# Sparse attention and a maxout layer on one core: a branch hint for ScalarE, an earlier check of the sums, and another order of work

## The chip, the cores and the metric

The kernel runs on one core of a Trainium2 chip. The metric is the device time of one execution, in microseconds; three runs of the kernel before gave 179.23, 179.29 and 179.44, and their median is the time before.

The core has a matrix engine (TensorE, PE in the profile; its weight loads are PEld), a vector engine (VectorE, DVE), an engine for functions of one operand (ScalarE, ACT), a general one (GpSimd, POOL) and one that issues transfers (SyncE, SP). Each has a sequencer of its own that takes its instructions in program order (PEq, DVEq, ACTq, POOLq and SPq in the profile). They meet through semaphores.

## The reference

Four batches of eight heads of 768 positions and 64 columns. Three heads see all earlier keys, the other five only the first four keys and the last 64. Then a layer of two products, the larger of both, and a third product:

```python
scores = scale * np.matmul(q, k.transpose(0, 1, 3, 2))
...
mask = np.where(retr[0, :, 0, 0, None, None], full_mask, stream_mask)
scores = np.where(mask[None, :, :, :], scores, -1000000000.0)
scores = scores - np.max(scores, axis=-1, keepdims=True)
a = np.exp(scores)
a = a / (np.sum(a, axis=-1, keepdims=True) + 1e-09)
return np.matmul(a, v).astype(np.float32)
...
h1 = x @ w1
h2 = x @ w2
g = np.maximum(h1, h2)
return (g @ w_out).astype(np.float32)
```

q, k, v and the result are float32; x has 3072 rows of 512, w1 and w2 are 512 x 1024, w_out is 1024 x 512.

## The kernel before

**Stages.** A batch is worked in two halves of 384 queries, in the order (batch, half) = (0,0), (1,0), (0,1), (1,1), (2,0), (2,1), (3,0), (3,1), and the eight heads of a batch in four pairs. For each half the loads bring q, k and v in float32. Casts (`cast_qk`, `cast_v`) make bfloat16 of them, picking the heads in an order that the chip works out from `is_retrieval` (`head_order`, L1578 to L1606) and keeps in registers. PE or a transposing DMA turns q and k (`turn`, L674), a copy takes them out (`unturn`). `mix_k` and `mix_v` lay out the first and the near keys of a window together (tiles `kx`, `vx`). Score tiles (`scores`, L953) go to PSUM, ACT takes the exponential (`exp`, L972), DVE the mask (`mask`, L991), PE the products with v and a column of ones that gives the row sums (`weighted`, L1016). `normalise` multiplies by the inverse sums (`rez`; L1033 and L1043) into the tile `x`, which is turned to `xt`.

The layer uses max(h1, h2) = relu(x (w1 - w2)) + x w2: `sub` makes w1 - w2 (L1178), w2 w_out is folded into one matrix on the chip (L1195 turns w2, L1222 multiplies), `up` makes x (w1 - w2) in eight groups of columns (L1245, four matmuls each), `relu` follows (L1270, L1272), and `down` adds x w2 w_out and the relu's product with w_out (L1302, three groups of four matmuls for a tile of 128 rows). A copy takes the tile out (`ot`) and a DMA stores it (L1327). The very last piece, 128 columns wide, is copied and stored by ACT, the others are stored by SP.

**Order.** All this is a list of 1094 numbered operations. The string `PLAN` says in which order they are emitted and on which engine: `1092p4` is operation 1092 on PE with PSUM bank 4, `v` is DVE, `a` ACT, `g` POOL, `s` SP, and `x0*3` are three warm-up matmuls on zeros into bank 0 (tile `warmer`, L366). Each engine takes its own operations in this order and waits, in order, for what they need.

**The numbers used below.** Loads on SP: 3 and 8 are the two halves of w2, 13 and 16 those of w1, 4, 6, 9 and 11 the four quarters of w_out. 52 is a cast of q and 38 one of v's rows in half (0,0). 237, 241, 244 and 249 are the first four score tiles of half (1,0), 174, 176, 188, 190, 202 and 204 their `mix_k`, 201 an `unturn`. 206, 208, 210, 212, 217, 219, 221 and 223 are the ups of half (0,0); 208 and 221 are the first, in the plan before and in the other, that need the half of w1 which is loaded last. 214 is a `down` group of it. 989 to 991 and 979 to 981 are `down` groups of half (3,0), 992 the copy behind 991. 1081 to 1088 end half (3,1), 1089 and 1090 are ACT's last copy and store.

**The check.** Operations 1091 to 1093 test that all inverse sums are sane and that three heads see everything: `judge` (four instructions on DVE), `total` (one matmul of one column on PE) and `say` (three on DVE), which writes `verdict`. Every engine loads `verdict` into a register and branches: with a verdict of 1 past `tile_any_heads`, a slow version that covers any heads and that this input does not need, to the end of the program. There the engines meet, SP waits for all semaphores one by one, and a barrier ends the program (both at L1727 of the profile). For some engines the branch has a hint: an instruction at their start that names the branch's target as likely.

Of the kernel before, what the change touches and what calls it, by code (L numbers as in the profile page):

```python
# [177 lines left out]
100p 94p3 101v 96p 104p0 102v 106p 14s 139p 103v 107v 138p 97v 109v 141p 98v 142p 108v 15s 99v 150p 126v 116p2
114p4 117a 151p 115v 134p6 137p 12v 217p0 130v 145p 218a 152p 146a 219p3 17s 118v 153a 223p2 220a 122v 221p4
224a 208p0 222v 18s 192a 180g 212p1 154a 164g 178v 209a 210p5 194v 156a 213v 184p3 160p2 211a 166v 198p4 185v  # L180
140p 143p 199v 21s 155a 167g 147p 165a 157g 179v 144a 195g 172p0 162p1 161v 170p5 181a 193g 206p3 19s 163a
173v 148a 200p4 174v 186p6 171a 237p21 201v 420s 241p07 187a 176v x5*2 204v x5*2 243a x5 207v 244p54 238a x6
249p67 188v 216p3 190v 245a 202v 250a 247v 242a 227p 239a 20s 251a 240v 234p 246a 252v 248v 421s 196a 182g
253p25 197a 158v 257p60 169a 159g 261p17 215p4 254a 168v 255a 203v 175v 265p2 177a 256v 259a 266p 270p5 226p
23s 258a 267v 205v 268v 262a 260v 183a 231p 263a 235a 191v 264v 271p 276p0 189v 232a 236s 281p 214p6 272v 269v
295a 289g 423s 282v 305v 306a 296g 275p1 284v 277p 225p 283v 315g 424s 274v 290g 309p7 316v 228p 310a 278v 22s
273v 279v 319p3 229a 311v 293p4 280v 299p2 320a 313v 294v 287p0 285p5 288a 323v 356p76 286v 422s 360p13 357a
363p40 321v 335p5 300v 361a 670s 450g 433a 337p7 441g 427v 442a 358a 325p1 301v 303v 434a 446v 24s 338a 359v
339p2 438g 326a 428v 331p6 365a 336v 340a 327p7 332v 449a 364a 333p1 454g 328v 669s 426a 439g 341p0 440v 432a
425g 362a 334v 329p5 547s 448v 431v 366p26 447v 330a 369p47 374p31 368a 550s 297v 307g 292v 429p5 370a 317g  # L190
451p6 291v 375a 435p4 298g 668s 371a 452v 342p 308g 430a 302g 343p 373v 312g 376a 453v 367a 393p3 394p 344a
304g 436v 395p 318a 396p 377p76 324a 322g 549s 381p51 372v 385p20 379a 346p4 383a 437v 380v 314v 386a 672s
397v 347p 399v 382a 398v 230s 378a 389p61 384v 233s 387a 348p 391a 388v 390a 400p2 401p 407p5 392v 402p 406p3
403v 351p7 803s 579a 568v 558g 404v 559a 405v 412p 578g 569a 408p 562p0 413v 409v 552a 673s 414v 352p 563a
415v 411v 548s 353p 553a 410v 349a 418p1 354a 556p6 350s 419v 416p2 557a 800s 486p50 417v 490p34 488a 493p71
443p6 491a 457p2 444v 495a 675s 459p0 494a 458v 487a 455p3 460v 671s 492a 469p1 445v 456v 345s 496p67 489v
470a 499p25 504p04 497a 507p31 501a 806s 523p6 564v 498a 524p 566v 503v 525p 506a 526p 467p5 551s 505a 527v
529v 509a 463p7 528v 500a 468v 461p4 807s 684g 677a 683v 700g 464a 465p0 510v 355s 462a 692g 476p1 508a 502v
699a 678g 688s 466v 511p62 691a 515p57 513a 519p43 477p 681s 555v 581g 517a 516a 580g 530p0 554g 560a 531p
518v 561g 696s 532p 521a 481p2 520a 533v 535v 570g 512a 482p 522v 695s 571a 514v 565a 537p7 542p 572p5 689v  # L200
585a 587g 543v 534v 536p3 802s 538p 545v 582p4 573a 539v 483p 544v 540v 583a 676s 574v 478p 541v 577a 484v
575a 619p60 546s 584v 623p75 479a 626p43 567v 586v 471p2 576v 620a 697v 625a 472p 628a 621a 687s 630v 473p
624a 622v 627a 631p16 703s 629v 635p53 632a 639p07 474v 652p4 633a 641a 647p1 634v 648p 643p62 640a 649v 653p
651v 645a 804s 594p7 654v 644a 650v 637a 596p0 656v 674s 636a 655v 600p2 646v 595a 638v 597a 598p6 682s 601a
642v 590p1 599a 602p3 591v 592p4 926s 603v 657p5 593a 659p 480s 588p7 660v 661v 614p0 485s 702a 701g 680v 693a
679g 475s 589a 685v 609p2 706g 686a 704s 662v 694a 690a 738p61 698g 742p34 739a 745p75 801s 610p 746a 743a
611p 747a 744a 799s 658p6 663p 615p 740a 664v 665v 612a 924s 741v 616p 705v 666v 748p73 617v 751p54 749a
756p12 667s 752a 759p60 604p7 760a 754v 758a 824v 834g 605p 805s 808a 809v 814a 825g 606p 613s 815v 835a 757a
812s 775p5 750a 607v 776p 753a 777p 778p 763p62 761a 755v 767p13 779v 765a 771p74 762v 782p0 781v 772a 828s
783p 780v 719p2 773a 768a 707p5 774v 813s 816g 720a 721p7 811v 826a 817g 810a 708v 715p4 827a 818s 836a 821g  # L210
722v 833a 733p1 716a 831v 837v 823a 819s 769a 717p2 843v 841a 770v 784p 713p5 764a 785v 718v 839s 789p7 714a
794p 787v 709p4 795v 766v 711p3 829s 710a 797v 796v 788p6 712a 790p 786v 723p2 608s 791v 820v 792v 838s 734p
822v 793v 840v 842v 875p54 925s 879p73 882p06 877a 735p 880a 881a 928s 832v 830v 876a 724p 883a 878v 725p 884a
885v 736a 886v 798s 903p4 726v 904p 887p73 891p50 905v 888a 895p61 906v 908p2 892a 907v 728p7 897a 927s 893a
899p54 729p 889a 894v 900a 932s 901a 890v 896a 730p 902v 727s 898v 909p 913p1 731v 915p 914p0 929s 854p3 916v
910v 917v 919p 865p5 912v 911v 930s 920v 848p4 855v 922v 844p6 931s 921v 849a 918v 858p7 845a 732s 850p2 859a
856p3 923s 955a 934v 956g 933a 852p0 857v 940g 947a 846p4 948a 938s 853a 870p1 851a 847v 939a 935v 949g 937s
871p 957v 936a 942a 958a 950v 872p 941v 954a 962v 946g 866p 873v 944s 867p 973p6 868a 943s 994p73 974v 998p02
995a 1001p41 975p5 952s 996a 945v 1003a 977p6 997v 1000a 951s 976v 965p7 1002a 971p3 999a 966v 978a 967p1 960s
972v 1004p25 968v 969p4 1006a 959s 953v 1005a 1007p07 970v 1012p63 1009a 1015p15 737s 1019p24 1008a 1011v  # L220
1031p7 874s 1017a 1032p 1010v 1033p 1014a 618s 1018v 1034p 961v 984p0 1013a 869s 1035v 1036v 1016a 1037v
# [1410 lines left out]
def kernel(  # L1632
# [13 lines left out]
    nc = tc.nc  # L1646
# [9 lines left out]
    with tc.tile_pool(name="consts", bufs=1) as consts:  # L1656
# [13 lines left out]
        if K_BY_ACT:  # L1670
# [7 lines left out]
            found, engines=[nc.gpsimd.engine, nc.vector.engine, nc.scalar.engine], min_val=0, max_val=H - 1,  # L1678
# [8 lines left out]
        right = nc.values_load(  # L1687
            verdict, min_val=0, max_val=1, skip_runtime_bounds_check_because="a product of two flags"
        )
# [42 lines left out]
```

## Time and profile before

| | us |
|---|---|
| median of three runs | 179.29 |
| the profiled execution | 179.4 |
| its span, first to last instruction | 177.7 |
| PE busy in it | 169.6 |
| ACT busy | 124.5 |
| DVE busy | 117.0 |
| POOL busy | 32.5 |

The span is what the trace shows; 1.7 us of the execution lie around it. Busy times count work on data, and not a sequencer's branches, loads of registers, waits and issues of DMAs. Those stand in the groups by line under the engine's name with a q. TensorE's granted clock is 0.995 of full speed as a mean over the span. A row of the timeline gives the start, the length, engine, line and operation, and in brackets the idle time before it and what ended that.

### The profile page before, as it was taken

The numbers are of one execution on the slowest core, as the hardware profiler recorded it, in microseconds if no ns is written. First come the engines' busy times: TensorE is split into PE (matmuls) and PEld (weight loads), VectorE is DVE, ScalarE is ACT, GpSimd is POOL, SyncE is SP. The second block draws the span as 40 slices with busy tenths as digits, with TensorE's granted clock in tenths as the row PEclk, the third lists the DMA queues.
The fourth block names the chain that finished last, engine by engine and source line by source line (L and its number), as shares of the span: only waits on it lengthen the run. The fifth ranks groups of instructions, "written<-read, shape, count | busy, mean of one in ns | idle before, by whom it ended". The sixth has DMA issues, their size and how long they took to land.

```text
span 177.7 us, 4887 instructions
## 1 busy us (share of the span) xinstructions
PE 169.6 (95%) x1781; PEld 102.6 (58%) x1781; DVE 117.0 (66%) x326; ACT 124.5 (70%) x279; POOL 32.5 (18%) x80
## 2 busy tenths in 40 slices
PE   7999999999999999999999999999999999999970
PEld 7855655655756656666566447555554566545440
DVE  5448799878898787776777175786855578503130
ACT  3598716999698999999996879948475877132210
POOL 6860200320427310071001122000030000000000
PEclk9999999999999999999999999999999999999998
DMA  5999999999899998995959997549993261333040
GB/s 133 334 373 386 392 375 325 221 309 281 217 251 246 267 310 214 243 247 74 154 117 250 209 186 196 71 115 223 226 252 71 66 220 66 76 131 118 4 160 28
DMA packets 76654, 36.14 MB, mean 203 GB/s; under 512 B 59090, under 2 KB 70610, under 8 KB 76626
## 3 DMA queue, kind: packets, MB, share of 16 engines
q1 hardware_dynamic: 76480, 35.73, 78.5%
q8 instruction: 15, 0.25, 0.6%
q14 instruction: 13, 0.11, 0.2%
q10 hardware_dynamic: 146, 0.07, 0.1%
HBM read 25.17 MB, written 6.29 MB: 177 GB/s over the span
## 4 chain that ended last, share of the span: by engine, by line
PE 78%; DMA 7%; DVE 5%; ACT 2%; POOL 2%; issue 2%; DVEq 0%; SPq 0%; POOLq 0%; ACTq 0%
PE ps L1302 34%; PE ps L1245 21%; PE ps L953 9%; PE ps L1016 7%; DMA ld<-in_moe_w_out_dram 6%; PE ps L1222 3%; PE ps L674 3%; DVE at L991 1%; ACT at L972 1%; PE ps L1142 1%; POOL qb L378 1%; DMA raw<-in_is_retrieval_dram 1%; ACT wob L376 1%; POOL tab L606 1%; DVE vx L378 1%
## 5 line engine op out<-in xcount | busy, mean ns | idle before, releaser
L972 ACT ACTIVATE at<-ps 128x512 bf16<-128x512 f32 (+2 forms) x134 | 64.0, 576 | 6.7 <-PE ps L953 6.4
L1302 PE MATMUL ps<-wob,g 128*128 128x512 bf16 (+2 forms) x200 | 45.7, 371 | 0.0
L1245 PE MATMUL ps<-xt,w 128*128 128x384 bf16 x256 | 45.2, 326 | 0.0
L1245 PEld LDWEIGHTS <-w 128*128 128x128 bf16 x256 | 24.1, 98 | 16.5 <-issue 0.6
L991 DVE TENSOR_TENSOR at<-at,tab 128x1024 bf16<-128x1024 bf16 (+5 forms) x49 | 24.7, 519 | 12.4 <-ACT at L972 11.8
L1302 PEld LDWEIGHTS <-g 128*128 128x128 bf16 x200 | 18.2, 98 | 19.4 <-issue 0.2
L1272 DVE TENSOR_SCALAR g<-ps 128x384 bf16<-128x384 f32 x31 | 16.9, 552 | 14.7 <-PE ps L1245 14.3
L1302 PE MATMUL ps<-w2o,xt 128*128 128x512 bf16 (+2 forms) x100 | 24.7, 371 | 0.0
L1270 ACT ACTIVATE g<-ps 128x384 bf16<-128x384 f32 x33 | 15.9, 509 | 12.0 <-PE ps L1245 11.9
L1043 DVE TENSOR_TENSOR x<-ps,rez 128x192 f32 x64 | 22.6, 354 | 1.6
L378 POOL CAST qb<-ld 128x384 bf16 (+1 forms) x28 | 12.4, 476 | 57.3 <-DVE x L1043 19.8
L1016 PEld LDWEIGHTS <-at 128*128 128x128 bf16 x477 | 18.0, 97 | 6.1 <-DVE at L991 1.0
L376 ACT COPY ot<-ps 128x512 f32<-128x512 f32 (+1 forms) x16 | 9.1, 576 | 16.4 <-PE ps L1302 15.4
L1016 PE MATMUL ps<-vb,at 128*128 128x65 bf16 x387 | 19.3, 193 | 0.3 <-DVE at L991 0.2
L953 PE MATMUL ps<-qk 64*128 64x128 bf16 (+1 forms) x330 | 19.1, 228 | 0.0
L953 PEld LDWEIGHTS <-qk 64*128 64x128 bf16 x330 | 12.1, 94 | 9.3 <-issue 7.0
L376 ACT CAST qb<-ld 128x384 bf16 (+1 forms) x35 | 13.7, 451 | 4.5 <-DMA ld<-in_q_dram 3.3
L1302 PEld LDWEIGHTS <-xt 128*128 128x128 bf16 x100 | 8.9, 98 | 8.1
L378 DVE COPY qk<-ps 128x384 bf16<-128x384 bf16 (+1 forms) x14 | 9.6, 696 | 4.0 <-PE ps L674 3.6
L378 POOL CAST vb<-ld 128x192 bf16 x18 | 6.3, 385 | 28.7 <-DMA ld<-in_v_dram 26.6
L378 DVE COPY ot<-ps 128x512 f32<-128x512 f32 (+1 forms) x9 | 6.1, 673 | 8.0 <-PE ps L1302 8.0
L674 PE MATMUL ps<-tab,qb 128*128 128x128 bf16 x120 | 9.6, 219 | 0.5 <-POOL qb L378 0.3
(76 smaller groups left out, 162.9 us busy)
## 6 DMA issues: line engine op xcount, KB each, us to landing
out_dram<-ot SPq DMA_DIRECT2D x23, 256.0 KB, 2.6
ld<-in_v_dram SPq DMA_DIRECT2D x21, 256.0 KB, 5.2
ld<-in_moe_w_dram SPq DMA_DIRECT2D x4, 1024.0 KB, 12.1
ld<-in_q_dram SPq DMA_DIRECT2D x5, 768.0 KB, 8.2
ld<-in_k_dram SPq DMA_DIRECT2D x5, 768.0 KB, 7.8
ld<-in_q_dram SPq DMA_DIRECT2D x9, 256.0 KB, 5.1
ld<-in_k_dram SPq DMA_DIRECT2D x9, 256.0 KB, 4.6
ld<-in_moe_w_out_dram SPq DMA_DIRECT2D x4, 512.0 KB, 11.0
```

The costliest lines, as they stand in the source:

```text
L376: nc.scalar.copy(out=out, in_=in_)
L378: eng[e].tensor_copy(out=out, in_=in_)
L674: nc.tensor.transpose(to[:, i], qbs[:, T["qb", n, hf] % NQB, t, i].rearrange("p h d -> p (h d)"), ident)
L953: nc.tensor.matmul(to.rearrange("p (i c) -> p i c", c=128), lhsT=lhsT, rhs=q_of(n, i, m)[rows], start=bk not in under, stop=True, skip_gro ...
L972: nc.scalar.activation(out=at[:, bk, 0:w], in_=bank(("ps", b, hf, t), part=bk)[:, 0:w], func=ACT.Exp, scale=scale,)
L991: eng[e].tensor_tensor(out=at, in0=at, in1=tbl, op=ALU.mult)
L1016: nc.tensor.matmul(po[:, hh, i - NT * hf, :], lhsT=ats[:, T["at", b, hf, t] % NAT, bk, e * 128:(e + 1) * 128], rhs=rhs, start=first, stop= ...
L1043: nc.vector.tensor_tensor(out=xs[:, HALVES.index((b, hf)) % NX, :, bass.ds(heads[2 * p + hh], 1), :], in0=po[:, hh, :, 0:D].unsqueeze(2), ...
L1245: nc.tensor.matmul(bank(key)[:, 0:HALF], lhsT=w[:, kc, fc * 128:(fc + 1) * 128], rhs=xts[:, HALVES.index((b, hf)) % NXT, :, kc, :], start= ...
L1270: nc.scalar.activation(out=g, in_=ph, func=ACT.Relu)
L1272: nc.vector.tensor_scalar_max(out=g, in0=ph, scalar1=0.0)
L1302: nc.tensor.matmul(bank(key)[:, cols], lhsT=lhsT, rhs=(w2o if kind == "x" else wob)[:, c, cols], start=(e == 0), stop=(e == len(steps) - 1),)
```

## The change

The hint is given to ScalarE's branch as well. `total` and `say` are emitted between the product groups of half (3,0) instead of behind the last products. The rest of `PLAN` is another order of the same 1094 operations, with other engines for 113 of the casts, copies and relus, other PSUM banks, and 81 warm-up matmuls instead of 87. Nothing else differs. The diff, cut to its first lines, the lines around the first score tiles of half (1,0) and its end:

```diff
@@ -170,60 +170,60 @@
 PLAN = """
-0s x0*3 1s x0*5 2s x0*40 8s 52a 54v 62g x0*3 32a x0 56p0 60a 25g x1*2 30a 57v x1 68g 64p1 70a x2 48p2 29g 65v
-x3 72p3 49a 73v x4*2 28g x4*6 3s 31a x4 53g x4*4 33a x4 69g x4*3 4s 71a x4*2 55g x4 50p4 63a x5 74p5 61g 51a
-58p6 26g x7*2 66p7 75a 59v x0 76p01 67a 27g 79p23 9s 36a 37v 40g 78a 35v 6s 38a 82p45 34v 81a 39v 85p67 41v
-80a 83a 46p1 86a 16s 127v 44p3 87a 11s 131v 84a 128p2 45a 47v 42p4 77a 129v 132p6 43a 88p75 133v 13s 119v
...
-173v 148a 200p4 174v 186p6 171a 237p21 201v 420s 241p07 187a 176v x5*2 204v x5*2 243a x5 207v 244p54 238a x6
-249p67 188v 216p3 190v 245a 202v 250a 247v 242a 227p 239a 20s 251a 240v 234p 246a 252v 248v 421s 196a 182g
...
-1038p5 1020a 1039p 1040p 1021a 1023p36 1041v 1027p17 1042v 1025a 963p2 1022v 1029a 860p4 1043v 1028a 964v
-1024a 1044p6 1030v 985p 1026v 1046p 986p 1047v 1048v 1049v 1045p7 1050p 989p5 1051v 1052v 1053v 990p 1054s
-1091v 991p 979p1 992a 993s 980p 981p 861p 982a 983s 862p 1061p2 863a 1067p3 864s 1062a 1071p6 1068a 1055p7
-1081p5 1056v 1059p1 1057p4 1060v 1063p2 1058v 987a 1069p3 1064v 988s 1065p7 1070a 1076p1 1066a 1072p 1077p
-1078p 1073p 1079v 1082p 1080s 1074a 1083p 1075s 1086p4 1084v 1087p 1088p 1092p0 1085s 1089a 1093v 1090a
+0s x0*3 1s x0*5 2s x0*40 3s 30a 32v 68g x0*3 70a 54v x0 48p0 62a 27g x1 72p1 49v x2*4 29g 60a 73v x2 64p2 x3*2
+65a x3*2 52g x3*5 8s 31a 55v x3 61g x3*2 56p3 33a 53v x4*3 4s 63a x4*2 69g x4 50p4 71a 57v x5 66p5 51a 58p6
+28g x7 74p7 67a 59v x0*2 26g 76p01 75a 25g 79p23 9s 34a 37v 78a 36v 6s 35v 39a 82p45 77a 41g 85p67 84a 40a
+88p10 83a 86a 13s 119v 91p54 38a 123v 89a 11s 46p6 87a 93a 42p1 47v 92a 44p7 80a 43v 16s 124p4 81a 127v 120p6
...
+223p7 161v 155a 157g 218a 185v 181g 172p6 162p0 195g 179a 206p5 224v 173a
+193g 17s 163a 174v 186p4 200p1 176v 187a 207v 237p23 241p76 420s 201v x0 239a 244p04 214p5 190v 242a 204v 188v
+245a 202v 238a 225p 247v 243a 240v 246a 249p13 20s 253p70 251a 257p26 248v 216p4 250a 252v 254a 423s 169v 168g
...
+1021a 1023p56 1041v 1027p42 1042v 1025a 963p0 1022v 1029a 860p1 1043v 1028a 964v 1024a 1044p6 1030v 985p 1026v
+1046p 986p 1047v 1048v 1049v 1045p2 1050p 989p3 1051v 1052v 1053v 990p 1054s 1091v 991p 1092p4 979p0 992a
+1093v 993s 980p 981p 861p 982a 983s 862p 1061p5 863a 1067p6 864s 1062a 1071p2 1068a 1055p3 1081p0 1056v 1059p1
+1057p5 1060v 1063p6 1058v 987a 1069p4 1064v 988s 1065p3 1070a 1076p1 1066a 1072p 1077p 1078p 1073p 1079v 1082p
+1080s 1074a 1083p 1075s 1086p5 1084v 1087p 1088p 1085s 1089a 1090a
 """
@@ -1683,7 +1683,7 @@
         tc.mark_branch_hint_location("other", hint="LikelyTaken",
-            engines=[nc.tensor.engine, nc.vector.engine, nc.gpsimd.engine])
+            engines=[nc.tensor.engine, nc.vector.engine, nc.gpsimd.engine, nc.scalar.engine])
         right = nc.values_load(
```

More of the change, by code (lines that the diff above doesn't have):

```diff
@@ L172 @@
 PLAN = """
-0s x0*3 1s x0*5 2s x0*40 8s 52a 54v 62g x0*3 32a x0 56p0 60a 25g x1*2 30a 57v x1 68g 64p1 70a x2 48p2 29g 65v
-x3 72p3 49a 73v x4*2 28g x4*6 3s 31a x4 53g x4*4 33a x4 69g x4*3 4s 71a x4*2 55g x4 50p4 63a x5 74p5 61g 51a
-58p6 26g x7*2 66p7 75a 59v x0 76p01 67a 27g 79p23 9s 36a 37v 40g 78a 35v 6s 38a 82p45 34v 81a 39v 85p67 41v
-80a 83a 46p1 86a 16s 127v 44p3 87a 11s 131v 84a 128p2 45a 47v 42p4 77a 129v 132p6 43a 88p75 133v 13s 119v
-91p31 90a 123v 89a 120p0 5v 93a 124p2 92a 121v 105p4 95p6 125a 10g 110p 149p5 111v 136p7 113v 112v 135p1 7a
@@ L178 @@
[L178 to L181, printed above, removed]
-173v 148a 200p4 174v 186p6 171a 237p21 201v 420s 241p07 187a 176v x5*2 204v x5*2 243a x5 207v 244p54 238a x6
@@ L183 @@
-249p67 188v 216p3 190v 245a 202v 250a 247v 242a 227p 239a 20s 251a 240v 234p 246a 252v 248v 421s 196a 182g
[L184 to L221, printed above, removed]
-1038p5 1020a 1039p 1040p 1021a 1023p36 1041v 1027p17 1042v 1025a 963p2 1022v 1029a 860p4 1043v 1028a 964v
@@ new lines @@
+65a x3*2 52g x3*5 8s 31a 55v x3 61g x3*2 56p3 33a 53v x4*3 4s 63a x4*2 69g x4 50p4 71a 57v x5 66p5 51a 58p6
+28g x7 74p7 67a 59v x0*2 26g 76p01 75a 25g 79p23 9s 34a 37v 78a 36v 6s 35v 39a 82p45 77a 41g 85p67 84a 40a
+88p10 83a 86a 13s 119v 91p54 38a 123v 89a 11s 46p6 87a 93a 42p1 47v 92a 44p7 80a 43v 16s 124p4 81a 127v 120p6
+45a 131v 128p5 125a 104p2 121v 106p 94p1 90a 96p 107v 5v 95p3 10g 100p 132p7 109v 105p4 97v 101v 110p 108v
+135p6 98v 149p0 111v 99v 7a 136p2 113v 134p1 103v 14s 138p 112v 133v 139p 150p 129v 137p 15s 122v 142p 151p
@@ new lines @@
+141p 12g 102v 140p 118v 116p4 114p7 143p 117v 115a 152p 145p 153a 147p 18s 130v 146a 212p5 144a 208p3 126v
+213a 148a 221p4 209v 210p7 19s 154a 178g 192a 194g 166v 219p0 211a 156v 164v 198p6 180v 160p1 170p5 199a 220v
+217p2 171a 222v 184p3 21s 165a 167g 223p7 161v 155a 157g 218a 185v 181g 172p6 162p0 195g 179a 206p5 224v 173a
+193g 17s 163a 174v 186p4 200p1 176v 187a 207v 237p23 241p76 420s 201v x0 239a 244p04 214p5 190v 242a 204v 188v
+245a 202v 238a 225p 247v 243a 240v 246a 249p13 20s 253p70 251a 257p26 248v 216p4 250a 252v 254a 423s 169v 168g
@@ new lines @@
+183a 227p 197a 196g 255a 175g 205v 177a 234p 182a 158a 256v 258a 261p31 228p 191v 259a 189v 421s 203v 263a
+260v 159a 275p7 262a 270p0 235a 265p2 264v 271p 266p 229a 276p6 236s 272v 267v 281p 274v 277p 215p1 268v 24s
+306a 289g 290v 305a 316g 226p 273v 295a 269v 315g 296a 424s 278v 309p3 282v 279v 231p 310a 284v 283v 23s 293p4
+280v 319p5 311v 294a 313v 287p0 232v 285p2 320a 299p3 288v 356p67 286v 360p41 357a 363p05 422s 300v 339p2 358a
+365a 323v 329p6 359v 22s 450g 442a 441v 337p7 364a 230s 427v 361a 333p3 434v 547s 321v 340a 433v 325p5 362a
@@ new lines @@
+301v 334v 449a 327p0 303v 326a 438v 454g 330v 428a 331p4 338a 328v 446a 335p2 233s 431g 448v 426a 440g 366p13
+332a 447v 369p56 374p70 367a 432g 551s 307v 318a 341p4 376a 425g 668s 336v 368a 451p1 375a 439g 308v 342p 298a
+291g 371a 452v 312g 343p 370a 317g 373v 800s 377p03 297g 324a 381p27 453v 385p61 378a 314g 351p5 302v 382a
+292g 322a 372v 435p0 549s 383a 393p2 436v 394p 344a 304g 429p7 387a 395p 548s 384v 400p4 386a 396p 401p 437v
+430a 389p01 397v 388v 406p6 669s 391a 352p 399v 398v 390a 407p7 379a 392v 353p 380v 408p 402p 354a 675s 553v
@@ new lines @@
+568g 412p 346p1 409v 403v 569a 413v 411v 559g 558a 405v 347p 552g 670s 579a 414v 578a 410v 556p2 404v 348p
+415v 672s 557a 418p0 349a 562p3 419v 671s 416p5 563a 486p64 417v 490p72 350s 488a 493p10 443p3 495a 455p5 444v
+802s 491a 457p4 494a 456v 487a 469p0 673s 458v 492a 465p7 445v 489v 470a 496p31 550s 466a 499p56 504p42 498a
+507p07 500a 463p1 564v 508a 566v 502v 509a 467p5 464v 804s 501a 459p0 510v 506a 468v 461p7 503v 497a 676s 678g
+460v 700a 523p1 505a 692g 462v 524p 525p 699g 691v 683a 806s 526p 511p65 561a 570g 515p23 555a 581v 519p07
@@ new lines @@
+345s 512a 684g 481p4 527v 696s 560v 521a 516a 571g 529v 476p6 528v 517a 580v 520a 530p7 677v 531p 518v 695s
+513a 532p 582p2 522v 565a 572p1 583a 537p3 514v 682s 477p 573a 533v 586v 534v 542p 536p0 535v 688s 587g 538p
+478p 543v 576v 577a 575g 539v 544v 482p 540v 807s 541v 585g 554a 545v 483p 479v 574v 546s 619p52 567v 484a
+584v 623p17 626p03 697v 471p6 624a 628a 689v 704s 625a 630v 472p 627a 620a 629v 473p 355s 621a 674s 622v
+631p41 652p3 633a 474v 635p70 632a 639p52 634v 636a 643p14 647p6 640a 653p 648p 803s 598p7 654v 649v 641a 656v
@@ new lines @@
+609p5 655v 644a 480s 645a 705v 651v 637a 590p2 650v 703s 599a 642v 588p1 591a 638v 596p3 681s 685a 680g 694v
+686a 702g 679a 658p4 646v 589a 657p0 594p6 693a 475s 701a 698v 690a 659p 706v 592p7 597a 660v 595v 687s 663p
+600p2 662v 593a 664v 661v 602p1 601a 799s 665v 666v 614p3 603a 926s 738p67 742p02 739a 745p41 610p 485s 743a
+801s 744a 611p 746a 740a 615p 612a 741v 616p 747a 924s 748p60 617v 751p24 667s 749a 756p75 752a 759p13 775p6
+761a 776p 754v 604p2 757a 762v 750a 805s 809v 825g 605p 824a 814v 835a 815g 613s 758a 606p 828s 808g 760a 753a
@@ new lines @@
+777p 778p 763p37 607a 755v 767p05 779v 834a 771p14 781v 782p2 819s 765a 780v 783p 768a 784p 711p7 785v 769a
+787v 838s 817g 709p6 786v 811a 816g 836a 770v 821g 713p0 823a 772a 812s 837v 715p5 764a 826a 714v 707p2 841a
+810g 818s 822v 820v 717p1 716a 843v 766v 708a 719p3 710a 718v 813s 773a 789p0 827v 721p5 712v 720a 831v 833a
+723p2 774v 608s 839s 722v 788p6 790p 794p 733p1 791v 795v 792v 829s 796v 724p 797v 793v 725p 928s 875p47 726a
+879p35 882p06 734p 881a 883a 925s 842v 840v 884a 885v 735p 876a 798s 832v 886v 877a 830v 728p2 736v 880a 878v
@@ new lines @@
+887p50 891p64 889a 895p73 932s 903p1 892a 890v 904p 908p0 896a 905v 729p 907v 893a 927s 906v 888a 730p 894v
+897a 727s 898v 909p 899p67 913p4 901a 731v 914p1 900a 929s 854p5 910v 902v 912v 865p3 911v 930s 855v 915p 919p
+848p7 916v 920v 917v 844p6 922v 931s 849a 921v 858p2 918v 845a 732s 850p0 859a 856p5 923s 955a 934v 956g 933a
+852p7 940g 857v 947a 948a 846p1 938s 853a 870p4 851a 847v 939a 949g 935v 937s 871p 936a 942a 957v 958a 950v
+941v 872p 954a 962v 946g 866p 873v 944s 867p 973p6 868a 943s 994p25 974v 998p70 995a 1001p14 952s 975p3 945v
@@ new lines @@
+996a 1003a 977p6 997v 951s 1000a 976v 965p2 1002a 971p5 999a 966v 978a 967p4 960s 972v 1004p03 968v 969p1
+1006a 959s 953v 1005a 1007p72 970v 1012p65 1009a 1015p43 737s 1019p01 1008a 1011v 1031p2 874s 1017a 1032p
+1010v 1033p 618s 1014a 1018v 1034p 961v 984p7 869s 1013a 1035v 1036v 1016a 1037v 1038p3 1020a 1039p 1040p
+1021a 1023p56 1041v 1027p42 1042v 1025a 963p0 1022v 1029a 860p1 1043v 1028a 964v 1024a 1044p6 1030v 985p 1026v
+1046p 986p 1047v 1048v 1049v 1045p2 1050p 989p3 1051v 1052v 1053v 990p 1054s 1091v 991p 1092p4 979p0 992a
```

## The prediction

> **What bounds the kernel now.** I read the page first, then busy time by stretch, then the waits and the instructions of the last 6 us, then the places where the two orders differ. Page and stretches:
>
> ```profile
> span 177.7 us, 4887 instructions
> PE 169.6 (95%) x1781; PEld 102.6 (58%) x1781; DVE 117.0 (66%) x326; ACT 124.5 (70%) x279; POOL 32.5 (18%) x80
> ```
>
> ```profile
> 10.00:172.00 162.00, 161.21 (x1682) 94.82 (x1679) 112.01 (x299) 119.39 (x266) 24.78 (x55) 1.00 0.81 206
> 172.00:177.70 5.70, 0.00 (x0) 0.00 (x0) 0.43 (x3) 0.25 (x1) 0.00 (x0) 0.85 0.18 62
> ```
>
> The second fence gives a stretch, its length, then the busy time of PE, PEld, DVE, ACT and POOL. From 10 to 172 us PE is busy for 161.2 of 162.0 us: an order of the same products can win little there. From 172.0 to 177.7 us nearly nothing computes, yet 5.7 us pass. That stretch is the first place to look. The groups by line show the sequencers' instructions in it (count, then min/median/max ns, then first and last start):
>
> ```profile
> L1687 SPq TENSOR_LOAD <-verdict x1: 718/718/718, 172.6 to 172.6; - x1
> L1687 ACTq TENSOR_LOAD <-verdict x1: 555/555/555, 172.7 to 172.7; - x1
> ...
> L1690 DVEq COMPARE_BRANCH  x1: 84/84/84, 173.2 to 173.2; - x1
> L1690 ACTq COMPARE_BRANCH  x1: 54/54/54, 173.3 to 173.3; - x1
> L1690 SPq COMPARE_BRANCH  x1: 53/53/53, 173.4 to 173.4; - x1
> L1690 PEldq COMPARE_BRANCH  x1: 393/393/393, 173.4 to 173.4; - x1
> L1690 DVEq EVENT_SEMAPHORE  x1: 21/21/21, 173.9 to 173.9; - x1
> L1690 PEldq EVENT_SEMAPHORE  x1: 51/51/51, 173.9 to 173.9; - x1
> ...
> L1690 ACTq EVENT_SEMAPHORE  x1: 17/17/17, 176.7 to 176.7; - x1
> ```
>
> ```profile
> L1727 SPq EVENT_SEMAPHORE  x12: 28/28/1912, 174.2 to 174.9; - x12
> ```
>
> ```profile
> L1727 PEldq BRANCH_PREFETCH_HINT  x1: 50/50/50, 0.9 to 0.9; - x1
> ```
>
> ```profile
> SPq L1727 <- ACTq L1690: 1.9, 1, 1.9
> ...
> SPq L1687 <- DVE verdict L1399: 0.3, 1, 0.3
> ```
>
> Every engine loads the verdict, branches over the fallback and meets the others. Two of the hinted engines, DVE and PE, go on 0.7 us (173.2 to 173.9) and 0.5 us (173.4 to 173.9) after their branch began. ACT, not hinted, goes on 3.4 us after it (173.3 to 176.7). SP collects everybody in twelve waits from 174.2 on; all are short but the last, begun at 174.9, which stands 1.9 us for ACT. Then 1.0 us of barrier ends the span (176.7 to 177.7). So the end is set by ACT's jump, not by the check's arithmetic.
>
> **The hint on ACT.** Where ACT goes on like those two, it does so 0.5 to 0.7 us after 173.3, at 173.8 to 174.0. That is before SP's last wait begins (174.9), so that wait falls from 1.912 to 0.028 us: 1.9 us gone. Late next is SP's own row of twelve waits, which ACT would only overtake by taking more than 1.6 us (173.3 to 174.9). I take -1.9; the ends are 0 (no help) and -1.9, since SP's row caps it.
>
> The Trainium skill, "Runtime: NRT & Kernel Launch", section "Instruction fetch mechanics", says that a taken branch to code outside the current window stalls for a fetch, and that prefetch is purely sequential. The trace agrees on the stall (ACT, 3.4 us), but its hinted engines, in 0.5 to 0.7 us, speak against "purely". By the page's second half the hint would be worth nothing and the sum would lose its 1.9.
>
> The hint also costs ACT's queue 0.05 us at the start, as PE's does in the row above, ahead of the DMA that fetches is_retrieval. Its cover:
>
> ```profile
> 6.02 0.35 DVE L378 CAST qb<-ld 128x192 bf16 x1 [0.84 <-DMA ld<-in_q_dram]
> ```
>
> The head order would come 0.05 to 0.1 us later, but DVE stands 0.84 us for q's load after it. Cost 0; 0.1 with that cover gone.
>
> **The check ahead of the last products.** `total` (1092) moves on PE from the end to behind product group 991, and `say` (1093) on DVE to behind 992's place, ahead of its last relus. `judge` (1091) stays.
>
> ```profile
> 152.70 1.89 PE L1302 MATMUL ps<-wob,g 128*128 128x512 bf16 x8
> 152.93 0.25 DVE L1382 TENSOR_SCALAR ld<-rez 128x192 f32<-128x192 f32 x1
> ...
> 154.00 0.16 DVE L1385 CAST goodb<-good 128x1 bf16<-128x1 f32 x1
> 154.21 0.75 PEld L1302 LDWEIGHTS <-xt 128*128 128x128 bf16 x4
> 154.42 1.03 PE L1302 MATMUL ps<-w2o,xt 128*128 128x512 bf16 x4
> ...
> 171.91 0.33 SPq L1327 DMA_DIRECT2D out_dram<-ot  x1
> 171.98 0.27 ACT L376 COPY ot<-ps 128x128 f32<-128x128 f32 x1 [1.43 <-PE ps L1302]
> ...
> 172.28 0.38 ACTq L1327 DMA_DIRECT2D out_dram<-ot  x1
> ```
>
> And the chain of waits:
>
> ```profile
> 171.90 0.11 PE ps L1388
> ```
>
> `total` now waits on PE for `judge`, with 979 and all later products queued behind it. `judge` ends at 154.16 (154.00 + 0.16) and 979 began at 154.42, so it is in time by 0.26 us. `judge`, 989, 990 and 991 keep their relative places behind the last weighting, so this margin holds if the stages before slide. PE pays the 0.11 us of that row ahead of the last products instead of behind: the end of the products moves by +0.1 (0 to the 0.16 of that matmul). `say`, three short instructions, falls into time in which DVE waits; its price ahead is 0.
>
> What does it free? SP, POOL, DVE and PE loaded the verdict when `say` ended. SP's last store is issued by 172.24 (171.91 + 0.33) and its load began at 172.6, 0.3 us of it a wait for the verdict: that goes. ACT gains nothing: its own last DMA issue ends at 172.66 and its load already began at 172.7, so it will do so 0.1 later. As SP's row of waits now ends the kernel, I take -0.3 for its earlier start; the other end is 0, should the code behind SP's branch or the last output's landing hold it. No DMA is added, and SP's and ACT's last stores keep their order.
>
> **The new order of work.** Counted in the two plans: PE's 421 positions move by a mean of 2.6 and, `total` apart, by at most 18; the last 73 product groups keep their order. Of the casts, copies and relus 113 change engine, in all directions, so that ACT, DVE and POOL gain or lose a few in the whole span, and none of them is the bound. Three places have a price.
>
> First, the warm-up matmuls between the score tiles of half (1,0): six before, one after.
>
> ```profile
> 35.82 0.45 PE L366 MATMUL ps<-warmer 128*128 128x128 bf16 x5
> 35.91 0.42 DVE L378 COPY kx<-qk 64x128 bf16<-64x128 bf16 x2
> ...
> 36.21 0.28 PE L953 MATMUL ps<-qk 64*128 64x128 bf16 x3
> ...
> 36.54 0.23 PE L366 MATMUL ps<-warmer 128*128 128x128 bf16 x1
> ...
> 36.70 0.29 PE L953 MATMUL ps<-qk 64*128 64x128 bf16 x4
> ```
>
> The six hold PE for 0.39 (35.82 to 36.21) and 0.16 us (36.54 to 36.70), 0.55 together. They fill a wait for the mixed keys (second row). The new plan makes those of tile 2 (176) ahead of the unturning 201, and puts four products (214) where the second gap was. If the keys are in time, -0.45; if not, 0. I take -0.3.
>
> Second, PE's changes between score products and others: 26 runs of score tiles before, 25 after. From the chain of waits, eight products of one group behind a score run and behind another:
>
> ```profile
> 100.09 1.83 PE ps L1302 x8
> ...
> 117.38 1.73 PE ps L1302 x8
> ```
>
> 0.1 us for leaving such a run; one fewer, -0.1.
>
> Third, the loads: SP asks for w2's halves in the order 3, 8 instead of 8, 3, and for w1's 13, 11, 16 instead of 16, 11, 13. The first load of w_out now waits for cast 52, which stands on POOL behind two table steps, but it queues behind both halves of w2 as before. The halves are of one size, so what lands keeps its time and PE's work is swapped with it. Past 13 stands 11, which waits for the last cast of v's rows (38). That cast now stands on ACT behind three casts and five exponentials.
>
> ```profile
> 10.83 0.35 ACT L376 CAST xt<-ld 128x192 bf16 x1
> ...
> 11.82 3.04 ACT L972 ACTIVATE at<-ps 128x512 bf16<-128x512 f32 x6
> ...
> 14.75 1.68 SPq L541 DMA_DIRECT2D ld<-in_moe_w_dram  x1
> ```
>
> At 0.51 us each (3.04 / 6) and 0.35 for a cast it ends at 10.83 + 5 x 0.51 + 4 x 0.35 = 14.8 at the latest, as an estimate; 16 follows, when the last half was asked for before (14.75). Price 0; the late rival takes its other end.
>
> For the rest of the order I take 0. The most that it can win is PE's idle time in the stretch from 10 to 172 us (162.0 - 161.2 = 0.8); the nearest row for a new loss is the longest wait of PE's weight loads for another engine's result, in the waits.
>
> ```profile
> PEld L1016 <- DVE at L991: 1.0, 3, 0.6
> ```
>
> So -0.8 to +0.6 there.
>
> **The sum.** -1.9 (ACT's jump) -0.3 (SP's load) +0.1 (`total`) -0.3 (warm-ups) -0.1 (one change) = -2.5 us. The profiled execution took 179.4 us around its span of 177.7, so it becomes 176.9 with a span of 175.2. The median of the runs, 179.29, lies 0.1 below that execution: 176.8.
>
> **The rivals.** *The hint does not shorten ACT's jump.* Nothing of the 1.9 comes, and SP's earlier load only lengthens its wait for ACT. ACT starts 0.1 later by `total`; the order gives its -0.4: 179.29 - 0.3 = 179.0. For it: the hint stands 172 us ahead of the branch, and ACT runs 279 instructions in between. Against it: PE runs 1781 matmuls and DVE 326 instructions, and both went on in 0.5 to 0.7 us. The page of the Trainium skill named above gives this result. Chance 8%.
>
> *The order makes PE wait anew*, by up to the 0.6 us of the longest row, wins nothing with the warm-ups, and SP keeps its old start: -1.9 + 0.1 + 0.6 = -1.2, 178.1; half of that gives 177.6. For it: many casts change engine. Against: PE's positions hardly move. Chance 13%.
>
> *Slower: the second half of w1 comes late.* It is the last weight asked for, behind the wait for cast 38.
>
> ```profile
> 28.10 1.22 DVE L1178 TENSOR_TENSOR w<-ld 128x1024 bf16<-128x1024 f32 x1 [0.34 <-DMA ld<-in_moe_w_dram]
> ```
>
> ```profile
> 28.11 3.90 PE ps L1245 x24
> ```
>
> Before, the late half's first subtraction ran from 28.10 to 29.32. The second fence, from the chain, is six ups of 0.65; the fourth, 208, is the first to use that result, at 30.0. In the new plan up 221 is the first: ahead of it stand two ups fewer (2 x 0.65) and three folding steps more (3 x 0.43, two products of 0.216 each, from 1.73 for eight), the same work. The margin is 0.7 us. To end slower than before, the half must land over 3.2 us late (0.7 + the 2.5 won); at 3.7 late the time is 179.8. Against it: it was asked for 13 us before its use (14.75 to 28.10), so it stood behind older loads, and a request at about the same time meets the same queue. Chance 4%.
>
> **Chances and range.** Forecast, 176.0 to 177.5: 73%; the waits anew 13%; no help 8%; slower 4%; better than 176.0, 2%. Low end: -2.5 with the rest of the order at -0.8: 176.0. High end: the second rival's 178.1, taken as 178.2. That holds about 86%. About 0.2% (0.36 us) is what a measurement of this kernel can tell from no change. Half of the no-help case (below 178.93) counts as faster: faster 92%, same 4%, slower 4%.
>
> **What would show it.** Right: ACT's first instruction behind its branch at 0.5 to 0.7 us after it; twelve waits of SP at 28 ns; SP's load no longer released by the verdict; `total` behind 991 with no PE wait at L1388; a span near 175.2 of which the end behind the last product is about 3.6 us (5.8 before). Wrong: ACT still 3.4 us behind its branch; a wait of SP on a landing output; or PE idle by over 0.8 us between 10 and 172.

## The result, and the profile after

| | before | after |
|---|---|---|
| median of seven runs each, us | 179.44 | 178.08 |
| the profiled execution, us | 179.4 | 177.84 |
| its span, us | 177.7 | 176.0 |

The ratio of the two is 0.9918, with a 95% interval of 0.9892 to 0.9944: 1.4 us faster. On a second chip it was 0.9936 (0.9912 to 0.9959). The forecast was 176.8 with a range up to 178.2, so direction and range held, and 1.4 us of the 2.5 that were forecast came. The page of the changed kernel, and its busy time by stretch (stretch, length, PE, PEld, DVE, ACT, POOL, then granted clock, DMA share and GB/s):

```profile
span 176.0 us, 4862 instructions
...
PE 167.7 (95%) x1755; PEld 102.0 (58%) x1775; DVE 118.0 (67%) x327; ACT 123.7 (70%) x278; POOL 34.5 (20%) x80
```

```profile
10.00:172.00 162.00, 159.51 (x1655) 94.27 (x1672) 112.60 (x300) 118.84 (x266) 26.89 (x57) 1.00 0.80 206
172.00:176.00 4.00, 0.00 (x0) 0.00 (x0) 0.00 (x0) 0.12 (x1) 0.00 (x0) 0.99 0.23 75
```

Twenty matmul records are missing (x1755 against x1775 weight loads), so PE's lower busy time can't be read as idle time. The stretch from 172 us on, in which nearly nothing computes, went from 5.7 to 4.0 us. What the engines do at the branch (first and last start at the end of each row), and what SP waits for from 171 us on:

```profile
L1690 PEldq COMPARE_BRANCH  x1: 398/398/398, 170.6 to 170.6; - x1
...
L1690 DVEq COMPARE_BRANCH  x1: 90/90/90, 171.9 to 171.9; - x1
...
L1690 SPq COMPARE_BRANCH  x1: 53/53/53, 172.8 to 172.8; - x1
L1690 ACTq COMPARE_BRANCH  x1: 68/68/68, 173.2 to 173.2; - x1
L1690 ACTq EVENT_SEMAPHORE  x1: 17/17/17, 173.7 to 173.7; - x1
```

```profile
SPq L1727 <- DMA out_dram<-ot: 1.4, 1, 1.4
SPq L1327 <- DVE ot L378: 0.9, 1, 0.9
SPq L1727 <- PEq L1727: 0.7, 2, 0.5
```

ACT goes on 0.5 us behind its branch (3.4 before). SP's wait for ACT is gone. In its place stands a wait of 1.4 us for a store to land: the fifth of SP's twelve waits, and it ends at 174.7. By its semaphore the store is ACT's, the very last. The trace has 16 updates of that semaphore for this store: before, the 16th came 1.69 us behind ACT's issue, now it comes 2.50 behind it. PE now branches at 170.6 and DVE at 171.9, ahead of the issue of the last two stores (171.78 and 172.15) or just between them; before, every engine branched at 173.2 to 173.4. The transfers between 172 and 173 us (queue: packets, MB, share of the engines' time; then issues, with the median us to landing):

```profile
q1 hardware_dynamic: 98, 0.14, 37.1%
q8 instruction: 1, 0.02, 5.5%
...
out_dram<-ot SPq DMA_DIRECT2D x1, 192.0 KB, 2.7
```

q1 carries SP's stores, q10 ACT's. The row of q8 is one packet of 16 KB, a fetch of code for PE (it moves with PE's branch when PE alone is made late, below), which runs from 172.18 to 173.06. SP's store of 192 KB took 2.7 us to land; before it took 1.9:

```profile
out_dram<-ot SPq DMA_DIRECT2D x1, 192.0 KB, 1.9
```

That was the lead for the experiments.

### The profile page after: what moved, and what is told of

Read it like the earlier page. It is cut to its first block, busy times and chain, and to the rows that moved or that the text cites. A ratio compares the mean times of both kernels' runs of the same rounds, so it can differ in the third digit from the quotient of the medians.

```text
span 176.0 us, 4862 instructions
## 1 busy us (share of the span) xinstructions
PE 167.7 (95%) x1755; PEld 102.0 (58%) x1775; DVE 118.0 (67%) x327; ACT 123.7 (70%) x278; POOL 34.5 (20%) x80
## 4 chain that ended last, share of the span: by engine, by line
PE 69%; DMA 18%; ACT 4%; SPq 3%; issue 3%; DVE 2%; ACTq 0%; DVEq 0%
PE ps L1302 31%; PE ps L1245 21%; PE ps L953 7%; DMA ld<-in_moe_w_dram 7%; PE ps L1016 6%; DMA ld<-in_q_dram 6%; DMA ld<-in_v_dram 5%; PE ps L674 2%; ACT at L972 2%; SPq L436 1%; DVE w L1178 1%; PE ps L1142 1%; SPq L562 1%; SPq L449 1%; ACT ot L376 0%
## 5 line engine op out<-in xcount | busy, mean ns | idle before, releaser
L972 ACT ACTIVATE at<-ps 128x512 bf16<-128x512 f32 (+2 forms) x134 | 64.8, 578 | 4.6 <-PE ps L953 4.1
L1302 PE MATMUL ps<-wob,g 128*128 128x512 bf16 (+2 forms) x192 | 43.8, 370 | 0.7 <-issue 0.2
L991 DVE TENSOR_TENSOR at<-at,tab 128x1024 bf16<-128x1024 bf16 (+5 forms) x49 | 25.5, 531 | 12.5 <-ACT at L972 11.7
L1272 DVE TENSOR_SCALAR g<-ps 128x384 bf16<-128x384 f32 x34 | 18.4, 551 | 12.8 <-PE ps L1245 12.3
L1302 PE MATMUL ps<-w2o,xt 128*128 128x512 bf16 (+2 forms) x90 | 24.0, 370 | 0.5
L378 POOL CAST qb<-ld 128x384 bf16 (+1 forms) x31 | 13.6, 470 | 55.2 <-DMA ld<-in_k_dram 30.1
L1270 ACT ACTIVATE g<-ps 128x384 bf16<-128x384 f32 x30 | 14.5, 494 | 6.4 <-PE ps L1245 6.1
L376 ACT CAST qb<-ld 128x384 bf16 (+1 forms) x32 | 12.7, 449 | 3.9 <-DMA ld<-in_q_dram 3.0
L376 ACT COPY qk<-ps 128x384 bf16<-128x384 bf16 (+1 forms) x17 | 10.1, 630 | 1.7 <-PE ps L674 1.3
L378 DVE COPY qk<-ps 128x384 bf16<-128x384 bf16 (+1 forms) x11 | 7.5, 698 | 3.5 <-PE ps L674 2.2
```

Of the source, the lines that this page charges most:

```text
L376: nc.scalar.copy(out=out, in_=in_)
L378: eng[e].tensor_copy(out=out, in_=in_)
L972: nc.scalar.activation(out=at[:, bk, 0:w], in_=bank(("ps", b, hf, t), part=bk)[:, 0:w], func=ACT.Exp, scale=scale,)
L991: eng[e].tensor_tensor(out=at, in0=at, in1=tbl, op=ALU.mult)
L1270: nc.scalar.activation(out=g, in_=ph, func=ACT.Relu)
L1272: nc.vector.tensor_scalar_max(out=g, in0=ph, scalar1=0.0)
```

## The experiments

Below, *tail* is the time from ACT's issue of the last store to the end of the span, read from the traces: 5.41 us before (172.28 to 177.69), 3.88 after (172.15 to 176.02). It is free of the scatter ahead of it, which is large (last section). The theories: **A**, the early verdict lets PE and DVE jump while the last stores are in flight, and the code fetches that this starts delay a share of their packets; **B**, a landing takes some 2.5 us from its issue whatever the engines do, and now merely shows; **C**, the hint brings nothing. A ratio is always to the kernel before on the same chip. Of `PLAN`'s lines the diffs show only the places that differ. The first four kernels ran on one chip, where the kernel before took 179.63 us.

### The hint alone

```diff
-            engines=[nc.tensor.engine, nc.vector.engine, nc.gpsimd.engine])
+            engines=[nc.tensor.engine, nc.vector.engine, nc.gpsimd.engine, nc.scalar.engine])
```

> The plan of before, the check at the end, and the hint on ACT added: nothing else. Theory A (the early check harms the last store): with a late verdict all engines branch at about 173.2, the code that they fetch comes after the last store's packets, the store lands at about 174.1, and only ACT's wait of 1.9 us goes: 179.4 - 1.9 = 177.5, span 175.8, no SP wait for out_dram. Theory B (the landing of the last store takes 2.5 us from its issue, whatever the engines do): SP waits for it till 174.8 and then makes seven more waits; span about 176.2, time 177.9. Theory C (the hint is worth nothing): 179.4.

Measured: 177.87 us, ratio 0.9916 (0.9889 to 0.9943), tail 3.52. Its branch, and SP's waits:

```profile
L1690 ACTq COMPARE_BRANCH  x1: 68/68/68, 173.6 to 173.6; - x1
...
L1690 ACTq EVENT_SEMAPHORE  x1: 17/17/17, 174.1 to 174.1; - x1
```

```profile
SPq L1327 <- DVE good L1392: 1.2, 1, 1.2
SPq L1727 <- remote: 0.7, 1, 0.7
SPq L1727 <- PEq L1727: 0.7, 2, 0.5
```

C falls: the tail lost 1.89 us, the whole of SP's wait for ACT. And no wait for a landing stands in the list, though the stores are the same. By its time this run lies at B's 177.9 and not at A's 177.5, but that decides nothing: its products were 0.30 us later than in the trace of before, and were so already at the first score tiles of half (1,0).

### The early check alone

```diff
-1091v 991p 979p1 992a 993s
+1091v 991p 1092p0 979p1 992a 1093v 993s
-1088p 1092p0 1085s 1089a 1093v 1090a
+1088p 1085s 1089a 1090a
```

In this kernel `total` shares bank 0 with a product group of half (3,0), whose tile it overwrites; the instructions are the same in number.

> The plan of before with total behind 991 and say behind 992, no hint on ACT. ACT's jump still ends the kernel, 3.4 us behind its branch. A and B alike: the matmul of total costs PE 0.2 us (0.1 of its own and a wait for judge), nothing is won: 179.6. The prediction's own size was +0.1: 179.5.

Measured: 179.39 us, ratio 0.9972 (0.9953 to 0.9992), so a little faster than before, where 0.1 to 0.2 us slower was expected; tail 4.62. ACT took 2.6 us behind its branch in this trace (174.3 to 176.9), against 3.4, and that is all by which the tail is shorter (0.79). SP's waits and its last store:

```profile
SPq L1727 <- DMA out_dram<-ot: 1.5, 1, 1.5
SPq L1727 <- PEq L1727: 0.7, 2, 0.5
SPq L1727 <- ACTq L1690: 0.7, 1, 0.7
```

```profile
out_dram<-ot SPq DMA_DIRECT2D x1, 192.0 KB, 2.7
```

The slow landing comes with the early check, in the old order and without the hint.

### The new order alone, and with the hint

The changed kernel with `1092p4` and `1093v` put back to the end (`1088p 1092p4 1085s 1089a 1093v 1090a`); the first without the hint on ACT, the second with it.

> The new plan with total and say put back to the end, no hint on ACT. In the profile after, group 991 began 0.33 us earlier than before: 179.4 - 0.3 = 179.1 by that; by the prediction's size of the order (-0.4) 179.0; if the order is worth nothing, 179.4. ACT's jump still 3.4 us.

> The new plan with the hint, but with total and say at the end. Theory A: the early check was a loss of some 0.3 to 0.5 us on top of its 0.2 on PE: 177.5 - 0.3 = 177.2, faster than the changed kernel's 178.08; the last store lands before SP asks. Theory B: the landing holds SP as in the changed kernel, only PE's 0.2 comes back: 177.8.

Measured: 178.88 us, ratio 0.9966 (0.9947 to 0.9986), without the hint, and **177.16** us, ratio 0.9860 (0.9835 to 0.9885), with it; tails 4.94 and 3.58. Without the hint ACT took 2.9 us behind its branch, 0.5 less than before, and the tail is shorter by that. SP's waits, first without the hint, then with it, and with it the last stores:

```profile
SPq L1727 <- ACTq L1690: 1.4, 1, 1.4
SPq L1327 <- DVE good L1392: 1.3, 1, 1.3
SPq L1727 <- remote: 0.8, 1, 0.8
```

```profile
SPq L1327 <- DVE good L1392: 1.3, 1, 1.3
SPq L1727 <- remote: 0.8, 1, 0.8
SPq L1727 <- PEq L1727: 0.7, 2, 0.5
SPq L1687 <- DVE verdict L1399: 0.4, 1, 0.4
```

```profile
out_dram<-ot SPq DMA_DIRECT2D x1, 192.0 KB, 1.9
```

With hint and order the kernel is faster than the changed one by its ratio, 0.9860 against 0.9918, though on another chip: the third part of the change, the early check, costs time.

### The changed kernel and hint with order, again

> The changed kernel once more, for the comparisons of this chip. Its trace showed a fetch of 16 KB of code on the queue of PE at 172.18, 1.6 us behind PE's branch (170.6), and behind it a dozen packets of the last two stores one after another until 174.13; SP's 192-KB store took 2.7 us to land. 178.1 (177.5 to 178.7) and a wait of SP of 1.2 to 1.5 us for the last store's landing again, by all theories.

> Hint and new order, with the check left at the end, on the same chip as the changed kernel. Theory A (the early verdict lets PE jump while the last stores are in flight, and the fetch that this starts holds one DMA engine for 0.9 us): 0.5 to 0.9 below the changed kernel, the 192-KB store landing in 1.9 us. Theory B (a landing takes its time from the issue on, whatever the engines do): the difference between the two is only total's 0.2 us on PE, so 0.2 to 0.3 below.

Measured on a second chip (before 179.83): 178.54 us, ratio 0.9936 (0.9912 to 0.9959), tail 4.08; and 178.10 us, ratio 0.9900 (0.9863 to 0.9936), tail 3.58. The six runs of the second fell into two groups, 176.98 to 177.04 and 178.09 to 178.30, and the trace is of the lower. So the two differ by 0.4 us in time here, with overlapping intervals, and by 0.5 in the tail. SP's last store landed after 2.8 and 1.9 us.

### say behind DVE's last copy

```diff
-1093v 993s 980p
+993s 980p
-1088p 1085s 1089a 1090a
+1088p 1085s 1089a 1093v 1090a
```

> The changed kernel with total (1092) early on PE as it is, but say (1093) behind DVE's last copy, so that the verdict is known at about 172.3. Theory A: all jumps come behind 172.3, the 192-KB store lands in 1.9 us, SP does not wait for it, and the time is that of hint and order plus total's 0.2 and the 0.2 by which say is later: 0.4 above it, 0.3 to 0.5 below the changed kernel. Theory B: the wait of SP for the landing stays at 1.0 to 1.4 us, and the time is the changed kernel's within 0.2.

Measured: 2393.59 us. The span holds 18753 instructions instead of 4862: the verdict was not 1 and the slow version ran.

```profile
span 2390.7 us, 18753 instructions
```

`total` had left its sum in bank 4, and up 1069 took bank 4 long before `say` read it. The last kernel below differs only in the bank of 1069, and goes the fast way. Nothing on A or B.

### PE alone late

```diff
-1088p 1085s 1089a 1090a
+1088p x0*22 1085s 1089a 1090a
```

> The changed kernel with 22 warm-up matmuls on zeros behind PE's last product, so that PE alone jumps some 1.8 us later (about 172.4) while the verdict stays early for all others. Theory A, that it is PE's fetch alone: it starts behind 173.5, the stores are in by 173.5, the 192-KB store lands in 1.9 to 2.0 us, SP's wait for it falls from 1.4 to under 0.2 us, and the time is 0.5 (0.2 to 0.9) below the changed kernel unless PE, late itself, takes the landing's place. Theory A2, that the other engines' fetches (8 KB, at 173.2 and 174.3) do it: 2.5 to 2.7 us to land and the changed kernel's time. Theory B: the same as A2.

The 22 warm-ups move PE's branch from 1.57 us ahead of ACT's issue to 0.50 behind it, and the fetch on q8 goes with it, from +0.03 to +1.95 (a plus counts from ACT's issue of the last store). Measured: 178.34 us, ratio 0.9914 (0.9887 to 0.9942), tail 3.88: not 0.5 below the changed kernel. Its stores and SP's wait:

```profile
out_dram<-ot SPq DMA_DIRECT2D x1, 192.0 KB, 1.9
```

```profile
SPq L1727 <- DMA out_dram<-ot: 1.4, 1, 1.4
```

Half of A is shown, and half of A2. Without PE's fetch SP's store lands in 1.9 us again. But SP's wait for a landing stays. As in the changed kernel it is for ACT's store: DVE's fetch of 8 KB starts 1.08 us behind ACT's issue and ends at +1.66; from there on eight packets of ACT's store and one of 4 bytes follow one another, and the last ends at +1.88 instead of +1.31 as with hint and order. Of the 16 updates of its semaphore 15 came by +1.73, and the last at +2.51. In the changed kernel two were late, at +2.43 and +2.50. So PE's fetch delays SP's store, but taking it away alone leaves SP's wait where it was (it ends at +2.52 here, at +2.51 there).

### PE and DVE late

On top of the 22 warm-ups, two passes of DVE over the inverse sums, multiplied by 1, before it loads the verdict; the second kernel has `total` and `say` behind product group 980 besides. These and the next two ran on one chip (before 179.47).

```diff
+        for _ in range(2):
+            nc.vector.tensor_single_scalar(out=rez, in_=rez, scalar=1.0, op=ALU.mult)
         tc.mark_branch_hint_location("other", hint="LikelyTaken",
```

> The kernel of PE alone late (22 warm-up matmuls behind PE's last product), and DVE late too: two passes over the inverse sums, 128x192, multiplied by 1 in place, before DVE loads the verdict, about 0.55 us. Counted from ACT's issue of the last store, DVE's fetch of 8 KB (at +1.08 us in both traces of the changed kernel and of PE alone late) comes at +1.6, behind the last packet of an undisturbed store (+1.3, hint and order). Theory A (fetches of jumped engines hold a DMA engine in front of the store's last packets): packets end at +1.3, SP's wait for the landing ends at +1.9 instead of +2.5, the end of the span is +3.2 instead of +3.9: 0.6 to 0.8 below the changed kernel in the tail, and 0.2 below hint and order in all. Theory B (a landing takes 2.5 us from its issue): +2.5 and +3.9 as before.

> As the one before, and total (1092) and say (1093) one product group later, behind 980 instead of 991. If total's 0.20 us on PE was a wait of its weight load for judge, that wait is gone and 0.11 or less stays between 991 and 861 beside the products: 0.1 us below the one before in the trace from group 991 to group 861. If it is what one such matmul between two groups costs, 0.20 stays.

Measured: 177.19 us, ratio 0.9869 (0.9842 to 0.9897), and 177.34 us, ratio 0.9884 (0.9846 to 0.9922); tails 3.06 and 3.07. SP's wait in the first (its lines stand two further down):

```profile
SPq L1729 <- DMA out_dram<-ot: 0.6, 1, 0.6
```

DVE's fetch now starts at +1.49, behind the last packet (+1.31), and SP's wait ends at +1.70 instead of +2.51. The verdict was as early as in the changed kernel; only when PE and DVE jump differs. B falls; the trace of before spoke against it too, where ACT's store had landed at +1.69. DVE late with PE early was not tried, so how long PE's fetch alone would hold SP is not shown.

In the second kernel `total` still costs PE 0.20 us, from group 991 to group 861. The weight loads around `total` in the changed kernel, then in this one:

```profile
152.58 1.18 PEld L1302 LDWEIGHTS <-g 128*128 128x128 bf16 x6
154.18 0.08 PEld L1388 LDWEIGHTS <-goodb 128*1 128x1 bf16 x1 [0.42 <-DVE goodb L1385]
```

```profile
155.11 0.74 PEld L1302 LDWEIGHTS <-g 128*128 128x128 bf16 x4
156.28 0.08 PEld L1388 LDWEIGHTS <-goodb 128*1 128x1 bf16 x1 [0.42 <-issue]
```

The same 0.42 us of idle weight loading stands before it, though here `judge` was done 2 us ahead of it. So it is no wait for `judge`, whatever the first row names; it is the price of this matmul between two groups.

### Hint with order once more, and say late with a bank of its own

The second is the kernel that went the slow way, with `1069p7` for `1069p4`.

> Hint and order, check at the end, on the chip of the two before, as their measure. A tail of 3.58 us behind ACT's issue, as in both traces of it. Theory A: 0.2 to 0.3 above the two with PE and DVE late; theory B: 0.5 below them.

> The earlier kernel with say at the end took the slow version: total's sums stood in bank 4, which product group 1069 took before say read it. Here 1069 has bank 7. total early behind 991, say behind DVE's last copy: verdict some 0.5 us behind that copy. Theory A: all jumps are late, the 192-KB store lands in 1.9 us, SP does not wait for a landing, and the tail behind ACT's issue is 3.5 to 3.7 us (changed kernel 3.9 to 4.1). Theory B: SP's wait for the landing ends at +2.5 and the tail is 3.9.

Measured: 177.31 us, ratio 0.9874 (0.9844 to 0.9903), tail 3.57; and **176.97** us, ratio 0.9865 (0.9836 to 0.9895), tail 3.07. SP's waits in the second:

```profile
SPq L1727 <- PEq L1727: 0.7, 2, 0.5
SPq L1727 <- remote: 0.6, 1, 0.6
```

No wait for a landing: with jumps 0.4 to 0.8 us behind ACT's issue the fetches start at +1.54 and later. Its tail is 0.5 below that of hint and order, more than expected, since SP gets to its waits 0.6 us sooner behind the issue (+1.37 against +1.94). The four kernels of this chip can't be told apart by their times, whose intervals overlap; by the parts that don't scatter (tail, and 0.20 for `total`) this one is 0.3 below hint and order.

## Why the prediction was right, and where it was off

**The hint, -1.9: right.** Tail 5.41 to 3.52 with the hint alone. In the new order it took 1.37 (4.94 to 3.58), since ACT's jump without it was 0.5 shorter in that trace; with one trace each, whether that jump differs by kernel or by run is open. The medians give 1.8 and 1.7 us. The rival that the hint does nothing falls. The rule of the Trainium skill ("Runtime: NRT & Kernel Launch", "Instruction fetch mechanics") that prefetch is purely sequential does not hold for a hinted branch in these traces. The fetches of code between 170 and 178 us, first before, then with the hint alone:

```profile
q14 instruction: 4, 0.03, 1.5%
q8 instruction: 1, 0.02, 0.8%
```

```profile
q8 instruction: 1, 0.02, 1.1%
q14 instruction: 3, 0.02, 0.9%
```

q14 carries the fetches of 8 KB, and a packet does not say for which engine. By their times ACT fetches twice without the hint, once behind its branch and once behind its restart (177.34); with it, ACT goes on and one fetch is left.

**The early check, -0.3: the step that failed.** The prediction let SP start earlier and took 0 as the other end, "should the code behind SP's branch or the last output's landing hold it". SP did start earlier, and by more: its row of waits began 0.82 us behind ACT's issue instead of 1.89. All of that, and 0.3 more, went into the wait for ACT's store, which the prediction had named as a sign of being wrong ("a wait of SP on a landing output"). The landing did not only hold SP, it came later, at +2.50 instead of +1.69. The step counted the loads of the verdict that PE and DVE would make sooner, but gave their jumps no price, as engines with nothing left to do. In these traces a jump of PE or DVE is followed by a fetch of 16 or 8 KB 1.1 to 1.6 us later, and by then the last stores are on the DMA engines. Measured against hint and order (3.58) the tail grew by 0.30 and 0.50 us in the two traces, where -0.3 stood in the sum. Without the collision the early `total` is worth -0.5 (3.07); SP then passes at +1.70, with the landing at +1.69.

**`total` ahead, +0.1: 0.20.** The sum took 0.11 from the row at the end of the chain, where no product follows; between two groups the same matmul costs 0.20, as in the old order with the early check. The margin that the prediction guarded, 0.26 us for `judge`, is not what it hangs on.

**The order, -0.4: -0.24 shown.** By the weight loads, all eleven traces of the new order (the slow version's too) agree within 0.02 us from group 486 (70 us) to group 991, and so do the three of the old one; the new one is 0.24 shorter there. The waits of PE's weight loads from 70 to 172 us, before and then after, have one change to score products fewer (-0.1 in the sum) and no longer the waits for the mask:

```profile
PEld L953 <- issue: 4.2, 11, 0.4
PEld L1016 <- DVE at L991: 0.8, 2, 0.6
```

```profile
PEld L953 <- issue: 3.8, 10, 0.4
PEld L1388 <- DVE goodb L1385: 0.4, 1, 0.4
```

Which of the two gave how much of the 0.24 was not tried. The warm-ups, -0.3 in the sum, lie ahead of 486. After:

```profile
35.36 0.51 PE L953 MATMUL ps<-qk 64*128 64x128 bf16 x12
...
35.80 0.23 PE L366 MATMUL ps<-warmer 128*128 128x128 bf16 x1
...
35.97 0.28 PE L953 MATMUL ps<-qk 64*128 64x128 bf16 x3
```

By the weight loads the third score tile of half (1,0) (244) begins 0.60 us behind the first in every trace of the new order, and 0.83 in every one of the old: 0.23 shorter, so the keys were in time. The second gap was not won: the products put there (214) wait 0.16 us for a copy by DVE. Whether the 0.23 lasts is open, since at 486 the two orders can't be told apart: 69.88 to 70.98 us against 70.17 to 70.97.

**The sum** of the changed kernel's trace: -1.89 (hint), +0.06 (tail of hint and order against the hint alone), +0.30 (landing), +0.20 (`total`), -0.33 (PE's products at group 991) = -1.66, and the span fell from 177.7 to 176.0. The -0.33 is of this one pair of traces and holds their scatter. That the time lies in the range is partly luck: its high end, 178.2, was priced for another mechanism, and the 178.08 measured is just under it. The rival in which the order makes PE wait anew gave 177.6 to 178.1 (half its wait gives 177.8, 179.29 - 1.9 + 0.1 + 0.3, and not 177.6), near the time measured, but not by its mechanism: behind 70 us PE has no new wait but the 0.42 before `total`. The subtraction that was to be late with w1's second half began 0.2 us later than before (28.28), and no product waited for it.

## What to carry to other kernels

A hint for the branch is worth having on every engine on which the end waits; look at the time from the branch to the next instruction, engine by engine. Before an engine is released early, ask what its next fetch of code will meet: here PE, released 2.7 us sooner against ACT's issue, made SP's last store land 0.8 us later, which nothing waited for; DVE's fetch alone held ACT's last store, for which SP waits; and DVE held back by 0.5 us of useless work, with PE late as well, took 0.8 us off the tail. So look for the transfer on which the end waits, and not for the one that is latest against its usual time. A one-column matmul moved off the end into a row of products cost 0.20 us here, against 0.11 at the end.

## What the runs showed of the hardware

- In the changed kernel's trace PE's fetch of code of 16 KB took 0.88 us, DVE's of 8 KB 0.44, and most of a store's packets of 1536 bytes 0.065. Of the last two stores' packets 25 began from 173.48 on, when all others had ended, and the last ended at 174.14. They stand in two rows. One is six packets of SP's store and then eight of ACT's (512 bytes). The other is eight of ACT's from the end of DVE's fetch (173.67) on. Each closes with packets of 4 bytes. With PE alone late only the second row is left, and one late update of ACT's semaphore instead of two. The Trainium skill, "DMA: Bandwidth & Descriptors", section "Why a DMA increments its semaphore by 16 and not by 1", says that up to 16 engines share a transfer, finish independently, and that it has landed only when all have. The two rows fit that, as two engines, each with a backlog behind a fetch; the trace does not name the engine of a packet, so this is argued.
- SP passes its wait for ACT's store 0.4 to 0.65 us after the last packet's end (+1.31 to +1.70 with PE and DVE late, +1.99 to +2.51 in the changed kernel, +1.88 to +2.52 with PE alone late).
- Unhinted, ACT took 2.6, 2.9 and 3.4 us from its branch to its next instruction in three traces; hinted, 0.5 with the hint alone and in the changed kernel.
- The scatter between runs arises ahead of 70 us: up to 1.1 us between traces of one order there, and no more than 0.02 us from there to group 991. Its cause was not looked for.
